# Fused attention, MLP and expert layer: when the experts' weight buffers are asked for again, and two scatters without a wait between them

## The chip, the cores and the metric

One core of one Trainium2 chip. The metric is the device time of one execution in microseconds (us), lower is better. Everything is float32 at the inputs and outputs.

## The reference, cut to what matters

Attention with a block mask over 4 x 8 x 576 x 64 gives 2304 rows of 512. A dense layer (512 to 2048 to 512, PReLU) follows, and then the part in which the change lies: eight experts (512 to 1024 to 512, ReLU), of which each row visits the one with the largest logit.

```python
def _moe2_ref(x, w_gate, w1, w2):
    N, D = x.shape
    E = w_gate.shape[1]
    logits = x @ w_gate
    expert_idx = np.argmax(logits, axis=1)
    probs = np.exp(logits - logits.max(-1, keepdims=True))
    probs /= probs.sum(-1, keepdims=True) + 1e-09
    gate_w = probs[np.arange(N), expert_idx]
    out = np.zeros((N, D), dtype=np.float32)
    for e in range(E):
        mask = expert_idx == e
        if not mask.any():
            continue
        h = np.maximum(x[mask] @ w1[e], 0.0)
        out[mask] = gate_w[mask, None] * (h @ w2[e])
    return out
```

## The kernel before, in words

Attention and the dense layer fill the first 651 us of the profile; a planner (class `Plan`) orders their instructions, and the change does not touch it. The dense layer's results go to a DRAM tensor `x2`, 256 rows at a time in nine groups. After each group `Route` finds every row's expert, its place in that expert's list and its gate value, and POOL scatters (row number, gate value) into the DRAM tensor `info` with two indirect DMAs of 128 places each (`Route.scatter`, L853). The last group's routing runs inside the first expert tile: its steps stand in a dictionary that `Route.steps` returns (L878), by the number of half-finished products after which they are called.

`Experts.run` (L1156) takes the experts in order of size, r = 0, 1, 2, ... Expert r's rows come in tiles: `big(r, j)` does 256 rows (`tile256`, L1037), `remainder(r)` the rest with 128 or 64 rows, and `only(r)` an expert of at most 128 rows (`tile128`, L1066, or `tile64`, L1104). How many rows an expert has is known on the chip alone, so `tc.If` branches choose, and all five engines take each branch. In the profiled run the expert of rank 0 took tiles j = 0 to 4 and a remainder of 128, rank 1 two tiles and a remainder of 64, rank 2 one tile and a remainder of 64, rank 3 one tile of 128, rank 4 one of 64, and the rest had no rows.

For a tile, `fetch(r, j)` (L990) has SP load 256 entries of `info` into a small tile `it` (for j > 0 also into `rem`), and POOL gather the rows of `x2` that `it` names into `xg`, 128 rows per indirect DMA. `xprep` (L999) turns them with four transposes on PE (`Tx`) and splits them into a high and a low part (ACT copies, DVE subtracts: `cxh`, `cxl`). Then PE multiplies in three passes (`pass3`): first layer into `l` (or `H`), ReLU into `hh` and `hl`, second layer into `Y`, ACT scales it into `yo`, and POOL scatters `yo` to the output rows.

An expert's weights are 16 blocks of 128 x 512 float32, 256 KB each. SP loads them into 16 buffers `raw0` to `raw15` (`wload`, L970, its DMA at L977), and `conv(r, i)` (L984) makes a high part of a block on ACT and a low part on DVE (`e`). Blocks of the next expert but one are loaded while those of the next are converted: `load_next(r)` (L1179) asks for all 16 of expert r + 2 and stands behind the whole tile in which expert r + 1's blocks are converted. Each load waits until DVE has converted the block that is in the buffer. The conversions are jobs: a tile's `step` calls (L1017) take one or more of them between pieces of the products, and with `more=1` also one entry of the list `ahead`, which `nexts` (L1172) makes: the gathers' `xprep` of the next tile, the `fetch` of the next expert's first tile, and its `xprep`. A 256-row tile with jobs has 16 steps: eight in the first layer, four in each half of the second. `tile128` and `tile64` have few steps with several jobs each.

Rank 1's blocks are asked for by an entry of `ahead` in the first tile (L1257), which stands ahead of the branch `few0` (L1266; 640 rows or fewer) and the branch `many0` (L1273; more). SP runs its instructions in the order in which they are written. It waits at each for what that one needs, and all its DMAs go out on the one queue q1. Where a branch is not taken, the block that takes its place waits for the DMAs of SP's eight lanes that are under way.

Of the kernel before, what the change touches and what calls it, by code (L numbers as in the profile page):

```python
# [778 lines left out]
class Route:  # L779
# [53 lines left out]
    def place(A, rk):  # L833
        nc, K, g, GE, oh, ex, sm, small = A.nc, A.K, A.g, GT * E, A.oh, A.ex, A.sm, A.small
        run = K.run[g % 2]
        for i in range(GT):
            nc.vector.tensor_add(run[:, i + 1], run[:, i], rk[:, E * i:E * i + E])
        nc.vector.tensor_copy(K.run[(g + 1) % 2][:, 0], run[:, GT])
        pos, sl, A.si = small("pos", [GT, E]), small("sl", [GT]), small("si", [GT], I32)
        nc.vector.tensor_add(pos, run[:, 0:GT], rk[:, GE:2 * GE].rearrange("p (i e) -> p i e", e=E))  # L840
        nc.vector.tensor_mul(pos, pos, oh)
        nc.vector.reduce_sum(sl, pos, axis=AX.X)
        nc.vector.tensor_copy(A.si, sl)

        A.ig, gx, ge = small("ig", [GT, 2], I32), small("gx", [GT, E]), small("ge", [GT])
        nc.gpsimd.tensor_scalar(A.ig[:, :, 0], K.pid, g * G, None, op0=ALU.add)
        nc.vector.tensor_scalar_add(sm, sm, 1e-9)
        nc.vector.tensor_mul(gx, ex, oh)
        nc.vector.reciprocal(sm, sm)
        nc.vector.reduce_sum(ge, gx, axis=AX.X)  # L850
        nc.vector.tensor_mul(A.ig[:, :, 1].bitcast(F32), ge, sm)

    def scatter(A, i):  # L853
        A.nc.gpsimd.indirect_dma_start(out=A.ml.info, out_offset=IOA(ap=A.si[:, i:i + 1], axis=0), in_=A.ig[:, i, :], in_offset=None)

    def steps(A, psp, xts):
# [20 lines left out]

        return {2: turns, 4: pick, 7: rank, 8: lambda: (A.scatter(0), A.scatter(1))}  # L878

# [50 lines left out]
class Experts:  # L930
# [59 lines left out]
    def fetch(A, r, j, base, rows=NT + 1):  # L990
        it = A.itile(r, j)
        src = A.info[ds(base + 2 * P * j, 2 * P), :].rearrange("(h p) c -> p h c", p=P)
        A.nc.sync.dma_start(it, src)
        if j:
            A.nc.sync.dma_start(A.rem, src)
        for h in range(2):
# [69 lines left out]
    def tile128(A, n, W, it, x, step):  # L1066
# [21 lines left out]

        step(5)
        l1(0, range(4))  # L1090
        step(3)
        l1(1, (0, 1))
        turn(0)
        step(2)
        l1(1, (2, 3))
        Y = A.psp.tile("H", f"Y{n}")
        l2((0, 1))
        turn(1)
        step(7, 2)
        l2(range(2, 8))  # L1100
# [55 lines left out]
    def run(A, base, last, order, order_all):  # L1156
# [21 lines left out]

        def load_next(r):  # L1179
            if r < E - 2:  # L1180
                A.load_raws(r + 2, reg(0, r + 2, E - 1))

        def big(r, j, b, jobs=(), nb=None):
            more = A.TOP[r] > 2 * P * (j + 1)
# [3 lines left out]
            if more:  # L1188
                A.fetch(r, j + 1, b)
            A.body(r, j, 2 * P, jobs, nexts(r, j + 1, b if more else None, nb))  # L1190
            if jobs:
                load_next(r)

# [20 lines left out]
        def remainder(r):  # L1214
# [8 lines left out]
            sized(P if A.TOP[r] > 2 * P + 64 else 64, lambda k: n > P - 1 + k, go)  # L1223

        def only(r, nb):

            jobs = [lambda: A.fetch(r + 1, 0, nb)] + [lambda i=i: A.conv(r + 1, i) for i in range(16)] if r < E - 1 else []
            if r < E - 2:
                jobs[-1] = lambda: (A.conv(r + 1, 15), load_next(r))

            def go(size):
                hint(f"more{r}", ns[r] > P)
                A.body(r, 0, size, jobs, xpreps(r + 1, 0) if jobs else (), cond=ns[r + 1] > 0 if jobs else None)
# [21 lines left out]
        for f in [lambda: A.fetch(0, 1, base), order_all, known] + [lambda i=i: late(i) for i in range(FIRST, 16)]:  # L1255
            at[max(at) + 1] = f
        ahead = [lambda: None] * 2 + [counts, lambda: A.load_raws(1, hold["e1"]), lambda: None] + xpreps(0, 1)  # L1257
        A.body(0, 0, 2 * P, [], ahead, at)
# [3 lines left out]

        def convs(r):
            return [lambda i=i: A.conv(r, i) for i in range(16)]

        with A.tc.If(n0 <= 5 * P, label="few0"):  # L1266
            with A.tc.If(n0 > 3 * P) as c:
                big(0, 1, base, convs(1), nb)
            with c.Else():
                for f in [lambda: A.fetch(1, 0, nb)] + convs(1) + xpreps(1, 0) + [lambda: load_next(0)]:  # L1270
                    f()
            hint("many0", n0 > 5 * P)
        with A.tc.If(n0 > 5 * P, label="many0"):  # L1273
            big(0, 1, base)
            big(0, 2, base, convs(1), nb)
            bigs(0, 3, base)
        remainder(0)
        with ExitStack() as st:  # L1278
            for r in range(1, E):
                base = nb  # L1280
                st.enter_context(A.tc.If(ns[r] > 0))
                nb = reg(2, r + 1, (E - 1) * NT) if r < E - 1 else None
                jobs = convs(r + 1) if r < E - 1 else []
                with A.tc.If(ns[r] <= P, label=f"less{r}"):  # L1284
                    only(r, nb)
                if r < E - 1:
                    st.enter_context(A.tc.If(ns[r] + P * ns[r + 1] > P))
                with A.tc.If(ns[r] > P, label=f"more{r}"):  # L1288
                    big(r, 0, base, jobs, nb)
                    bigs(r, 1, base)  # L1290
# [3 lines left out]
def moe_kernel(tc, qk, v, qke, ve, w_in, w_out, alpha, w_gate, w1, w2, out):  # L1294
    nc = tc.nc
    with ExitStack() as ctx:
# [135 lines left out]
        ex.s = od.pl.tile([P, 256], F32, name="s")  # L1432
        todo = Route(ml, NG - 1, lambda i: ex.yo[i], {}).steps(banks, [ex.xg[:, i] for i in range(GT)])
        ex.run(hold["base"], todo, od, lambda: od.all(K.run[(NG - 1) % 2][0:1, GT]))
# [52 lines left out]
```

## Time and profile before

| what | value |
|---|---|
| median of 3 runs | 951.15 us (950.98 to 956.93) |
| the profiled execution | 951.48 us; its span from first to last instruction 949.7 us |
| mean granted TensorE clock | 0.976 |
| busy: PE, DVE, ACT, POOL | 94%, 53%, 43%, 31% of the span |
| experts' part | from 651.6 us on; last product ends at 936.6 us, last scatter starts at 937.9 us |

How to read it: a row of a timeline has the start, the duration, the engine, the line, the operation, output<-inputs and, in brackets, how long the engine was idle before and what ended that. "SPq" is SP's instruction queue: its duration is the issuing of a DMA, not its transfer. Names stand without buffer numbers, so `xg` is either half of the gathered rows and `raw` any of the 16 buffers. The row of a window has the busy time of each engine in it, the granted TensorE clock (1.00 is 2.4 GHz, 0.50 is 1.2 GHz), the mean busy share of the 16 DMA engines and GB/s.

### The profile page before, as it was taken

How to read it: one execution, taken by the hardware profiler on the slowest of the kernel's cores; microseconds unless marked ns; L12 is line 12 of the kernel's file. 1: busy time of each engine (PE TensorE's matmuls, PEld its weight loads, DVE VectorE, ACT ScalarE, POOL GpSimd, SP SyncE). 2: the span in 40 equal slices, each digit the busy share in tenths (PEclk: the TensorE clock that was granted, in tenths of full speed). 3: DMA queues.
4: the chain of work that ended last, by engine and by line, in shares of the span. 5: the costliest groups of instructions: out<-in, count | busy, mean ns of one | idle time of the engine just before them, and what ended most of it. 6: DMA issues, size and time to landing. Idle time of an engine off the chain costs nothing. (4 is left out here: it accounts for less than half of the span.)

```text
span 949.7 us, 17897 instructions
## 1 busy us (share of the span) xinstructions
PE 892.8 (94%) x6329; PEld 763.4 (80%) x6329; DVE 499.5 (53%) x1215; ACT 409.7 (43%) x1037; POOL 294.1 (31%) x312
## 2 busy tenths in 40 slices
PE   7999989999999999999999999999889998998884
PEld 6656658888888888888999999979778987988763
DVE  4999896657546555656434353546215211613450
ACT  7777765454455446454312121223215222523451
POOL 1555673323343432443222223241212111111110
PEclk9999999999999999999999999999999998998997
DMA  8981002312302122001001010043526211622551
GB/s 340 362 317 56 23 20 74 75 48 71 75 28 76 48 59 94 28 27 36 31 2 45 1 45 2 23 123 101 170 88 222 68 47 56 198 62 80 169 163 62
DMA packets 46267, 85.80 MB, mean 90 GB/s; under 512 B 12191, under 2 KB 18991, under 8 KB 46128
## 3 DMA queue, kind: packets, MB, share of 16 engines
q1 hardware_dynamic: 35264, 64.20, 20.7%
q0 software_dynamic: 4240, 11.56, 3.8%
q10 hardware_dynamic: 6624, 8.39, 2.5%
q8 instruction: 63, 1.03, 0.5%
q14 instruction: 76, 0.62, 0.2%
HBM read 70.85 MB, written 13.67 MB: 89 GB/s over the span
## 5 line engine op out<-in xcount | busy, mean ns | idle before, releaser
L693 PE MATMUL l<-xh,wi 128*128 128x256 f32 x1024 | 206.0, 287 | 0.0
L693 PEld LDWEIGHTS l<-xh,wi 128*128 128x128 f32 x1024 | 167.0, 191 | 4.2 <-issue 0.5
L721 PE MATMUL acc<-wo,gh 128*128 128x512 f32 x512 | 167.3, 408 | 0.0
L693 PE MATMUL l<-xl,wi 128*128 128x256 f32 x512 | 145.0, 283 | 0.1
L699 POOL TENSOR_TENSOR gl<-t,gh 128x256 fp32r<-128x256 f32 x103 | 78.5, 764 | 193.3 <-ACT gh L696 158.4
L671 DVE TENSOR_SCALAR t<-l,al 128x256 f32<-128x256 f32 x128 | 61.9, 484 | 141.6 <-PE l L693 136.1
L696 ACT CAST gh<-t 128x256 fp32r<-128x256 f32 x124 | 50.4, 406 | 186.1 <-DVE t L672 105.3
L529 POOL TENSOR_SCALAR P<-P,sm 128x256 f32<-128x256 f32 (+4 forms) x66 | 78.4, 1195 | 107.7 <-ACT gh L696 39.8
L721 PE MATMUL acc<-wo,gl 128*128 128x512 f32 x256 | 101.0, 394 | 2.8 <-POOL gl L699 2.8
L693 PEld LDWEIGHTS l<-xl,wi 128*128 128x128 f32 x512 | 97.8, 191 | 4.0 <-issue 0.5
L721 PEld LDWEIGHTS acc<-wo,gh 128*128 128x128 f32 x512 | 87.0, 191 | 11.3 <-issue 0.5
L478 DVE TENSOR_REDUCE nb<-S 128x1 f32<-128x256 f32 (+4 forms) x160 | 70.1, 477 | 40.2 <-PE S L455 25.9
L523 ACT COPY F<-PT 128x384 f32<-128x384 f32 (+2 forms) x124 | 57.6, 479 | 52.8 <-PE PT L518 51.5
L495 ACT ACTIVATE P<-S,nb 128x128 f32<-128x128 f32 (+3 forms) x128 | 67.0, 531 | 14.3 <-DVE nb L478 12.9
L518 PE MATMUL PT<-ident,P 128*128 128x128 f32 (+1 forms) x400 | 64.7, 281 | 6.4 <-DVE xo L572 3.9
L518 PEld LDWEIGHTS PT<-ident,P 128*128 128x128 f32 (+1 forms) x400 | 45.9, 141 | 20.0 <-issue 3.5
L721 PEld LDWEIGHTS acc<-wo,gl 128*128 128x128 f32 x256 | 48.2, 188 | 14.7 <-POOL gl L699 3.7
L1031 PE MATMUL l<-cxh,e 128*128 128x256 f32 x320 | 58.3, 282 | 1.0 <-ACTq L1266 1.0
L1031 PE MATMUL Y<-e,hh 128*128 128x512 f32 x176 | 57.2, 406 | 0.0
L672 DVE SCALAR_TENSOR_TENSOR t<-l,t 128x256 f32<-128x256 f32 x128 | 54.3, 425 | 4.4
L988 DVE TENSOR_TENSOR e<-raw,e 128x512 fp32r<-128x512 f32 x68 | 43.9, 686 | 21.4 <-ACT e L987 17.8
L562 PE MATMUL o<-F,v 128*64 128x128 f32 (+2 forms) x832 | 53.4, 264 | 0.0
(373 smaller groups left out, 1677.8 us busy)
## 6 DMA issues: line engine op xcount, KB each, us to landing
raw<-in_moe_w_dram SPq DMA_DIRECT2D x96, 256.0 KB
qk<-in_qk_dram SPq DMA_DIRECT2D x16, 608.0 KB
rawi<-in_moe_w_in_dram SPq DMA_DIRECT2D x16, 512.0 KB
rawo<-in_moe_w_out_dram SPq DMA_DIRECT2D x16, 512.0 KB
v<-in_v_dram SPq DMA_DIRECT2D x16, 320.0 KB
x<-y ACTq DMA_DIRECT2D x16, 256.0 KB
xr<-xT SPq DMA_DIRECT2D x7, 512.0 KB
qe<-in_qke_dram SPq DMA_DIRECT2D x8, 256.0 KB
```

The lines of the kernel that those rows point to most:

```text
L478: nc.vector.tensor_reduce(pl["nb", p, c][:, 2 * k + j:2 * k + j + 1], pl[Ss[j]][:, a:b], axis=AX.X, op=ALU.max, negate=True)
L495: nc.scalar.activation(pl[x][:, a:b], pl[Ss[j]][:, a:b], AF.Exp, bias=nb, scale=1.0, accum_out=pl["sm", p, c][:, 2 * k + j:2 * k + j + 1])
L518: nc.tensor.transpose(pl[t][0:w, k], pl[x][:, P * k:P * k + w], A.K.ident)
L523: f(pl[F][:, 0:n], pl[t][:, 0:n])
L529: (nc.gpsimd if on == "POOL" else nc.vector).tensor_scalar(y, y, pl["sm", p, c][:, k:k + 1], None, op0=ALU.mult)
L562: nc.tensor.matmul(y, lhsT=v[0:w, 2 * kc + h], rhs=f, start=kc == 0, stop=kc == c, skip_group_check=True)
L671: nc.vector.tensor_scalar(pl[out], x, 0.0, A.K.al[:, f:f + 1], op0=ALU.min, op1=ALU.mult)
L672: nc.vector.scalar_tensor_tensor(pl[out], x, 0.0, pl[out], op0=ALU.max, op1=ALU.add)
L693: nc.tensor.matmul(pl[l][:, 0:G], lhsT=a[:, c], rhs=b, start=k == 0 and j == 0, stop=k == 3 and j == 2)
L699: (nc.gpsimd if on == "POOL" else nc.vector).tensor_sub(pl[gl], pl[t], pl[gh].bitcast(F32))
L721: nc.tensor.matmul(pl[acc], lhsT=x[:, c], rhs=w, start=f == 0 and j == 0, stop=f == 15 and j == 2)
L1031: A.nc.tensor.matmul(ps, lhsT=x[a], rhs=w[b], start=first and q == 0, stop=last and q == 2)
```

## The change

Three edits, and one of numbers.

1. The last group's scatters. The row numbers of its second half are written between the two scatters (`token(1)`), the dependence of the second scatter on the first is taken away (both write `info`, at other places), and the loads of `info` for tile (0, 1) get a dependence on both scatters.
2. Rank 1's blocks (`load_raws(1, ...)`) are no longer asked for in the first tile but in `big(0, 1)` behind the branch, after that tile's `fetch`.
3. `load_next` is gone. Each job converts a block and asks at once for the block of the next expert but one in the same buffer (`convs`, `one`).
4. `tile128` takes its jobs in portions of 4, 1, 3 and 9 in place of 5, 3, 2 and 7, and two branch hints are set in other places; the branch behind `only` gets a label (`on`) and a hint.

```diff
--- before.py
+++ after.py
@@ -843,15 +843,21 @@
         nc.vector.tensor_copy(A.si, sl)
 
         A.ig, gx, ge = small("ig", [GT, 2], I32), small("gx", [GT, E]), small("ge", [GT])
-        nc.gpsimd.tensor_scalar(A.ig[:, :, 0], K.pid, g * G, None, op0=ALU.add)
+        if g < NG - 1:
+            nc.gpsimd.tensor_scalar(A.ig[:, :, 0], K.pid, g * G, None, op0=ALU.add)
+        else:
+            A.token(0)
         nc.vector.tensor_scalar_add(sm, sm, 1e-9)
         nc.vector.tensor_mul(gx, ex, oh)
         nc.vector.reciprocal(sm, sm)
         nc.vector.reduce_sum(ge, gx, axis=AX.X)
         nc.vector.tensor_mul(A.ig[:, :, 1].bitcast(F32), ge, sm)
 
+    def token(A, i):
+        A.nc.gpsimd.tensor_scalar(A.ig[:, i, 0:1], A.K.pid[:, i:i + 1], A.g * G, None, op0=ALU.add)
+
     def scatter(A, i):
-        A.nc.gpsimd.indirect_dma_start(out=A.ml.info, out_offset=IOA(ap=A.si[:, i:i + 1], axis=0), in_=A.ig[:, i, :], in_offset=None)
+        return A.nc.gpsimd.indirect_dma_start(out=A.ml.info, out_offset=IOA(ap=A.si[:, i:i + 1], axis=0), in_=A.ig[:, i, :], in_offset=None)
 
     def steps(A, psp, xts):
 
@@ -875,7 +881,14 @@
             A.rank(rk)
             A.place(rk)
 
-        return {2: turns, 4: pick, 7: rank, 8: lambda: (A.scatter(0), A.scatter(1))}
+        def scatters():
+
+            tc, A.sent = A.ml.tc, [A.scatter(0)]
+            A.token(1)
+            A.sent.append(A.scatter(1))
+            tc.declare_no_dep(A.sent[1].ins, A.sent[0].ins, reason="other places")
+
+        return {2: turns, 4: pick, 7: rank, 8: scatters}
 
 
 class Order:
@@ -990,9 +1003,12 @@
     def fetch(A, r, j, base, rows=NT + 1):
         it = A.itile(r, j)
         src = A.info[ds(base + 2 * P * j, 2 * P), :].rearrange("(h p) c -> p h c", p=P)
-        A.nc.sync.dma_start(it, src)
+        got = [A.nc.sync.dma_start(it, src)]
         if j:
-            A.nc.sync.dma_start(A.rem, src)
+            got.append(A.nc.sync.dma_start(A.rem, src))
+        for x in got if (r, j) == (0, 1) else ():
+            for y in A.last.sent:
+                A.tc.add_manual_dep(x.ins, y.ins.name, mybir.DependencyInfo(mybir.DependencyClass.Sync, mybir.DependencyReason.DATA), reason="places")
         for h in range(2):
             A.nc.gpsimd.indirect_dma_start(out=A.xg[:, h], out_offset=None, in_=A.x2[0:rows, :], in_offset=IOA(ap=it[:, h, 0:1], axis=0))
 
@@ -1086,17 +1102,17 @@
             for f in fs:
                 A.pass3(Y, [t[:, f % 4 // 2, P * (f % 2):P * (f % 2) + P] for t in A.hs[f // 4]], W[8 + f], f == 0, f == 7)
 
-        step(5)
+        step(4)
         l1(0, range(4))
-        step(3)
+        step(1)
         l1(1, (0, 1))
         turn(0)
-        step(2)
+        step(3)
         l1(1, (2, 3))
         Y = A.psp.tile("H", f"Y{n}")
         l2((0, 1))
         turn(1)
-        step(7, 2)
+        step(9, 2)
         l2(range(2, 8))
         nc.scalar.activation(A.yo[0], Y, AF.Copy, scale=it[:, 0, 1:2].bitcast(F32))
         A.scatter(A.yo[0], it)
@@ -1176,20 +1192,16 @@
                 fs += [lambda: None] * (6 - len(fs)) + xpreps(r + 1, 0)
             return fs
 
-        def load_next(r):
-            if r < E - 2:
-                A.load_raws(r + 2, reg(0, r + 2, E - 1))
-
-        def big(r, j, b, jobs=(), nb=None):
+        def big(r, j, b, jobs=(), nb=None, raws=None):
             more = A.TOP[r] > 2 * P * (j + 1)
 
             if A.TOP[r] > 2 * P * (j + 1) + P and (r, j) != (0, 1):
                 hint(f"rest{r}_{j + 1}", ns[r] > 2 * P * (j + 1) + P)
             if more:
                 A.fetch(r, j + 1, b)
+            if raws is not None:
+                A.load_raws(1, raws)
             A.body(r, j, 2 * P, jobs, nexts(r, j + 1, b if more else None, nb))
-            if jobs:
-                load_next(r)
 
         def bigs(r, j, b):
             if A.TOP[r] > 2 * P * j + P:
@@ -1222,14 +1234,25 @@
 
             sized(P if A.TOP[r] > 2 * P + 64 else 64, lambda k: n > P - 1 + k, go)
 
+        def convs(r):
+
+            e = reg(0, r + 1, E - 1) if r < E - 1 else None
+
+            def one(i):
+                A.conv(r, i)
+                if e is not None:
+                    A.wload(r + 1, e, i, A.raws[i])
+
+            return [lambda i=i: one(i) for i in range(16)]
+
         def only(r, nb):
 
-            jobs = [lambda: A.fetch(r + 1, 0, nb)] + [lambda i=i: A.conv(r + 1, i) for i in range(16)] if r < E - 1 else []
-            if r < E - 2:
-                jobs[-1] = lambda: (A.conv(r + 1, 15), load_next(r))
+            jobs = [lambda: A.fetch(r + 1, 0, nb)] + convs(r + 1) if r < E - 1 else []
+            if jobs:
+                jobs[-1] = lambda f=jobs[-1]: (f(), hint(f"more{r}", ns[r] > P))
 
             def go(size):
-                hint(f"more{r}", ns[r] > P)
+                hint(f"on{r}" if jobs else f"more{r}", ns[r + 1] > 0 if jobs else ns[r] > P)
                 A.body(r, 0, size, jobs, xpreps(r + 1, 0) if jobs else (), cond=ns[r + 1] > 0 if jobs else None)
 
             with A.tc.If(ns[r] <= 64) as c:
@@ -1254,24 +1277,21 @@
 
         for f in [lambda: A.fetch(0, 1, base), order_all, known] + [lambda i=i: late(i) for i in range(FIRST, 16)]:
             at[max(at) + 1] = f
-        ahead = [lambda: None] * 2 + [counts, lambda: A.load_raws(1, hold["e1"]), lambda: None] + xpreps(0, 1)
+        ahead = [lambda: None] * 2 + [counts] + [lambda: None] * 2 + xpreps(0, 1)
         A.body(0, 0, 2 * P, [], ahead, at)
         nb = hold["nb"]
         ns = hold["n"]
         n0 = ns[0]
 
-        def convs(r):
-            return [lambda i=i: A.conv(r, i) for i in range(16)]
-
         with A.tc.If(n0 <= 5 * P, label="few0"):
             with A.tc.If(n0 > 3 * P) as c:
-                big(0, 1, base, convs(1), nb)
+                big(0, 1, base, convs(1), nb, hold["e1"])
             with c.Else():
-                for f in [lambda: A.fetch(1, 0, nb)] + convs(1) + xpreps(1, 0) + [lambda: load_next(0)]:
+                for f in [lambda: A.fetch(1, 0, nb), lambda: A.load_raws(1, hold["e1"])] + convs(1) + xpreps(1, 0):
                     f()
             hint("many0", n0 > 5 * P)
         with A.tc.If(n0 > 5 * P, label="many0"):
-            big(0, 1, base)
+            big(0, 1, base, raws=hold["e1"])
             big(0, 2, base, convs(1), nb)
             bigs(0, 3, base)
         remainder(0)
@@ -1280,13 +1300,12 @@
                 base = nb
                 st.enter_context(A.tc.If(ns[r] > 0))
                 nb = reg(2, r + 1, (E - 1) * NT) if r < E - 1 else None
-                jobs = convs(r + 1) if r < E - 1 else []
                 with A.tc.If(ns[r] <= P, label=f"less{r}"):
                     only(r, nb)
                 if r < E - 1:
-                    st.enter_context(A.tc.If(ns[r] + P * ns[r + 1] > P))
+                    st.enter_context(A.tc.If(ns[r] + P * ns[r + 1] > P, label=f"on{r}"))
                 with A.tc.If(ns[r] > P, label=f"more{r}"):
-                    big(r, 0, base, jobs, nb)
+                    big(r, 0, base, convs(r + 1) if r < E - 1 else [], nb)
                     bigs(r, 1, base)
                     remainder(r)
 
@@ -1430,7 +1449,8 @@
         od.pl = ctx.enter_context(tc.tile_pool(name="raw", bufs=1))
         ex.rawtiles(od.pl, 16 - NR)
         ex.s = od.pl.tile([P, 256], F32, name="s")
-        todo = Route(ml, NG - 1, lambda i: ex.yo[i], {}).steps(banks, [ex.xg[:, i] for i in range(GT)])
+        ex.last = Route(ml, NG - 1, lambda i: ex.yo[i], {})
+        todo = ex.last.steps(banks, [ex.xg[:, i] for i in range(GT)])
         ex.run(hold["base"], todo, od, lambda: od.all(K.run[(NG - 1) % 2][0:1, GT]))
```

The order in which instructions stand on an engine, before and with the change, at three places. On POOL, in the first expert tile, the two scatters of the last group (`ig` holds row number and gate value, `si` the places); before:

```order
L846 TENSOR_SCALAR ig8_8078<-pid_90 128x2
L854 DMA info_60<-ig8_8078,si8_8073 18432x2 x2
L997 DMA xg_6016<-x2_58,it11_6014 128x512 x2
L1247 TENSOR_LOAD odri_8127
L1170 REGISTER_ALU
```

and with the change:

```order
L857 TENSOR_SCALAR ig8_8078<-pid_90 128x1
L860 DMA info_60<-ig8_8078,si8_8073 18432x2
L857 TENSOR_SCALAR ig8_8078<-pid_90 128x1
L860 DMA info_60<-ig8_8078,si8_8073 18432x2
L1013 DMA xg_6016<-x2_58,it11_6014 128x512 x2
```

One instruction of POOL came between the scatters; the gathers of tile (0, 1) follow as before.

On SP, in the branch `many0`, from tile (0, 2)'s fetch to the conversions in that tile; `it10`, `it11` and `it01` are the lists of tiles (0, 2), (0, 3) and (1, 0). Before (the 16 loads of rank 1's blocks stand ahead of the branch, and are not in this piece):

```order
L1273 COMPARE_AND_BRANCH
L993 DMA it10_6013<-info_60 128x2x2
L995 DMA rem_6015<-info_60 128x2x2
L993 DMA it11_6014<-info_60 128x2x2
L995 DMA rem_6015<-info_60 128x2x2
L993 DMA it01_6012<-info_60 128x2x2
L977 DMA raw0_6031<-in_moe2_w1_dram 128x512
L977 DMA raw1_6032<-in_moe2_w1_dram 128x512
```

With the change, first the end of the 16 loads, which now stand between the lists of (0, 2) and (0, 3), and then the place of `it01`:

```order
L990 DMA raw15_7979<-in_moe2_w2_dram 128x512
L1006 DMA it11_6014<-info_60 128x2x2
L1008 DMA rem_6015<-info_60 128x2x2
L990 DMA raw0_6031<-in_moe2_w1_dram 128x512
...
L990 DMA raw9_7973<-in_moe2_w2_dram 128x512
L990 DMA raw10_7974<-in_moe2_w2_dram 128x512
L1006 DMA it01_6012<-info_60 128x2x2
L990 DMA raw11_7975<-in_moe2_w2_dram 128x512
```

The list of the next expert's first tile stood ahead of all 16 loads, and now stands behind eleven of them (`raw0` to `raw10`). In tiles (1, 0) and (2, 0) the order is the same: before, `it` of the next expert and then `raw0`; now `raw10`, `it`, `raw11`.

On DVE, in `tile128` of rank 3 (`e0` is a converted block, `hl0` the low part of the first half of the hidden values); before:

```order
L988 TENSOR_TENSOR e0_3_7785<-raw3_6034,e0_3_7785 128x512
L1020 UNCONDITIONAL_BRANCH x2
L1020 COMPARE_AND_BRANCH
L988 TENSOR_TENSOR e0_4_7811<-raw4_7968,e0_4_7811 128x512
L988 TENSOR_TENSOR e0_5_7832<-raw5_7969,e0_5_7832 128x512
L988 TENSOR_TENSOR e0_6_7851<-raw6_7970,e0_6_7851 128x512
L1020 UNCONDITIONAL_BRANCH x2
L1083 TENSOR_TENSOR hl0_6024<-Th3_0_128+_0_14668,hh0_6023 128x512
```

and with the change:

```order
L1001 TENSOR_TENSOR e0_3_7785<-raw3_6034,e0_3_7785 128x512
L1036 UNCONDITIONAL_BRANCH x2
L1099 TENSOR_TENSOR hl0_6024<-Th3_0_128+_0_14756,hh0_6023 128x512
L1036 COMPARE_AND_BRANCH
L1001 TENSOR_TENSOR e0_4_7811<-raw4_7968,e0_4_7811 128x512
```

Ahead of `hl0` stood seven conversions, and now four.

## Rows read from the trace of the kernel before

**Rows 1.** The page: span, and part 1, busy time of each engine.

```profile
span 949.7 us, 17897 instructions
...
PE 892.8 (94%) x6329; PEld 763.4 (80%) x6329; DVE 499.5 (53%) x1215; ACT 409.7 (43%) x1037; POOL 294.1 (31%) x312
```

**Rows 2.** Waits of PE, 651 to 950 us: total, times, longest.

```profile
PE Tx L1004 <- DMA xg<-x,it: 6.8, 4, 4.1
...
PE Y_128+_14687 L1031 <- DVE hl L1083: 2.4, 1, 2.4
```

**Rows 3.** Timeline of PE: transposes of gathered rows, each expert tile's next.

```profile
676.75 0.63 PE L1004 MATMUL Tx<-ident,xg 128*128 128x128 f32 x4 [2.15 <-DMA xg<-x,it]
...
700.06 1.09 PE L1004 MATMUL Tx<-ident,xg 128*128 128x128 f32 x4 [4.10 <-DMA xg<-x,it]
...
727.68 0.30 PE L1004 MATMUL Tx<-ident,xg 128*128 128x128 f32 x1 [0.37 <-DMA xg<-x,it]
...
733.74 0.27 PE L1004 MATMUL Tx<-ident,xg 128*128 128x128 f32 x1
...
824.67 0.27 PE L1004 MATMUL Tx<-ident,xg 128*128 128x128 f32 x1
...
889.33 0.27 PE L1004 MATMUL Tx<-ident,xg 128*128 128x128 f32 x1
```

**Rows 4.** Timeline of POOL: the last scatters of places, gathers of rows.

```profile
662.42 1.06 POOL L854 DMA_INDIRECT info<-ig,si  x1 [11.81 <-DVE odnf L893]
666.30 1.26 POOL L854 DMA_INDIRECT info<-ig,si  x1 [2.82 <-DMA info<-ig,si]
673.37 0.98 POOL L997 DMA_INDIRECT xg<-x,it  x1 [5.81 <-DMA it<-info]
...
696.54 0.99 POOL L997 DMA_INDIRECT xg<-x,it  x1 [13.07 <-DMA it<-info]
...
720.67 0.97 POOL L997 DMA_INDIRECT xg<-x,it  x1 [0.30 <-issue]
...
817.68 0.95 POOL L997 DMA_INDIRECT xg<-x,it  x1 [14.11 <-PE Tx L1004]
...
833.63 0.99 POOL L997 DMA_INDIRECT xg<-x,it  x1 [3.50 <-SPq L1196]
```

**Rows 5.** Timeline of SP's queue: lists of places, and loads of weight blocks.

```profile
676.04 11.93 SPq L977 DMA_DIRECT2D raw<-in_moe_w_dram  x16
693.94 0.39 SPq L993 DMA_DIRECT2D it<-info  x1
...
718.10 0.37 SPq L993 DMA_DIRECT2D it<-info  x1
...
730.88 0.33 SPq L977 DMA_DIRECT2D raw<-in_moe_w_dram  x1
...
821.82 0.55 SPq L977 DMA_DIRECT2D raw<-in_moe_w_dram  x1
...
830.37 0.03 SPq L993 DMA_DIRECT2D it<-info  x1
...
886.47 0.33 SPq L977 DMA_DIRECT2D raw<-in_moe_w_dram  x1
```

**Rows 6.** Windows, tiles (0, 1) and (0, 3), two stretches after waits: engines' busy time, clock, DMA.

```profile
681.64:710.90 29.26, 25.16 (x152) 22.28 (x153) 4.48 (x7) 4.26 (x7) 3.99 (x4) 0.94 0.44 149
...
735.93:759.49 23.56, 23.56 (x156) 21.28 (x155) 6.46 (x11) 5.95 (x10) 3.99 (x4) 1.00 0.23 69
...
700.06:703.50 3.44, 3.44 (x11) 2.79 (x12) 1.02 (x2) 0.59 (x1) 0.00 (x0) 0.51 0.12 49
...
915.40:918.50 3.10, 3.07 (x10) 2.58 (x11) 1.17 (x2) 0.11 (x1) 0.00 (x0) 0.51 0.98 303
```

**Rows 7.** Timeline of DVE, the tile of 128 rows of rank 3.

```profile
910.46 4.31 DVE L988 TENSOR_TENSOR e<-raw,e 128x512 fp32r<-128x512 f32 x7 [3.36 <-ACT yo L1075]
914.69 0.69 DVE L1083 TENSOR_TENSOR hl<-Th_128+_0_14668,hh 128x512 fp32r<-128x512 f32 x1
```

## The prediction

> **What bounds the kernel now.** I read the page first. PE is busy for 94% of the span [rows 1], so the change can win only where PE stops, and loses wherever it makes PE stop. The waits of PE come next. In the experts' part one wait is larger than any other: transposes that wait for gathered rows, 6.8 us in four waits, the longest 4.1 [rows 2]. The only stop by conversions is one of 2.4 us at the low part of rank 3's hidden values [rows 2]; no stop is put down to a weight block that has not landed. The reader is to see in this that loading weights earlier is worth nothing by itself: the loads keep up with the conversions already, and no product waits for one.
>
> Then PE's timeline at those transposes [rows 3], and behind each of them POOL's gather [rows 4] and SP's list [rows 5], because the chain is list, gather, transpose. Tile (0, 1): 2.15 us of idle PE before the transpose at 676.75. Tile (0, 2): 4.10 us before 700.06. The windows give what the second stop cost in all: tile (0, 1), in which PE prepares (0, 2), took 29.26 us, where tile (0, 3), with the same products and no stop, took 23.56 [rows 6]. The difference, 5.70, is 4.10 of idle time and 1.6 of slow clock: right behind the stop the granted clock is 0.51, near the level of 1.2 GHz, for 3.44 us [rows 6], which loses 3.44 x 0.49 = 1.7.
>
> **The change part by part.** The scatters. The second starts at 666.30 after 2.82 us of waiting for the first one's landing [rows 4]. Without that wait and with one small instruction of POOL between, it starts about 0.5 us after the first ends at 663.48, near 664.0, so 2.3 us earlier. The list, the gather at 673.37 and the landing before 676.75 follow it one by one, so all move by 2.3. PE came to this transpose 2.15 us before the rows. The stop goes: -2.15 us (between -1.5, should the token's instruction take longer than I put, and -2.15). What is late next is PE itself.
>
> Rank 1's loads behind the branch. Before, SP issues 16 loads from 676.04 to 687.97, then stands at the branch not taken, and issues tile (0, 2)'s list at 693.94, six us later [rows 5]; the gather follows at 696.54 and the transpose waits until 700.06. With the change SP has nothing under way at the branch but two short lists, and asks for (0, 2)'s rows ahead of the loads. It can do that near 678 to 680; even at 684 the rows would land before PE comes to the transpose at 696. The stop and its slow clock go: -5.7 us (-4.1 to -5.8). The 16 loads now begin some 4 us later than 676.04. They took 18 us to the end of the wait at 693.94, so they would be complete near 698, and the first conversion of rank 1 comes in tile (0, 2), behind 710.90 less the 8 us gained, 703. This cover is 5 us; if it were gone, conversions and not PE would be late, and they have 25 us of that tile to catch up.
>
> Portions of `tile128`. Rank 3's tile had seven conversions ahead of `hl`, 4.31 us for seven [rows 7], 0.62 each. With four, `hl` comes 1.85 us earlier and most of the 2.4 us stop goes. The slow stretch behind it, 3.10 us at 0.51 [rows 6], is worth another 1.5. Two more conversions, 1.2 us, stand behind the second turn instead, on the engines for which the last tile of 64 rows waits. So 1.85 + 1.5 - 1.2 = 2.1 us gained (0.6 to 3.3). The hints and the label I put at nothing: the branches whose stops the waits show at ranks 1 and 2 are not those that get a hint.
>
> Refilling at once. Here the price lies. Before, SP had issued the next expert's list long before its rows were wanted: at 718.10 [rows 5], for a transpose at 733.74 [rows 3]. The gather then waited only for its buffer: POOL's at 817.68, for the transpose at 824.67, had been held by the previous transpose and not by a list [rows 3, 4]. With the change this list stands behind the load of block 10, which waits for conversion 10. In the trace of before the load of block 11 is what SP issued next behind that conversion, at 730.88, 821.82 and 886.47 [rows 5] in the three tiles with 16 steps, and the list takes its place. From a list's issue to its gather 2.6 us pass with nothing in front (693.94 to 696.54), and 3.3 with a block load just issued in front (830.37 to 833.63) [rows 4, 5]. From the gather's start to the transpose that it holds up 3.4 to 3.5 us pass (673.37 to 676.75; 696.54 to 700.06), and 7.0 where a burst of block loads runs beside it (720.67 to 727.68) [rows 3, 4]. There is a load in front, so I take 3.3; the loads behind it come one by one as conversions end and not in a burst, so I take 3.5. Rows are there 6.8 us after the list: at 737.7, 828.6 and 893.3. PE wants them at 733.74, 824.67 and 889.33 [rows 3]. It stands still for 3.9 us at each of the three. By the low ends (2.6 + 3.4) it would be 3.1, by the high ends (3.3 + 7.0) 7.4. Behind stops of 4.1 and 2.4 us the clock fell [rows 2, 6], so I add 1.7 at each; the bounds are nothing, as after the stop of 2.15, and 1.7. That is 3 x (3.9 + 1.7) = +16.8 us, from 9.3 to 27.3. Nothing covers it: the transposes stand in PE's own order, and the next products cannot pass them. The block loads themselves start at about the times they did, since conversions set these.
>
> A rule speaks against this edit too. The trace shows a list that came 0.7 us later with one load in front [rows 4, 5]. The Trainium skill, "DMA: Bandwidth & Descriptors", section "Queues, rings and completion order", says that each DMA engine takes the descriptors of one ring in ring order, so that a list would wait for every block asked for ahead of it on SP's queue. By that rule tile (0, 2), where eleven blocks would be asked for between 718 and 731, could have one more of them before the list, some 0.8 us by a rough estimate, and the sum would be 0.8 us higher. I keep the row's 0.7.
>
> The sum: -2.15 - 5.7 - 2.1 = -9.95 gained, +16.8 lost, so +6.85 on the profiled execution's 951.48 us (the span of 949.7 and 1.8 around it): 958.3. The median of the three runs is 951.15, 0.3 below it; I forecast 958.0 us, 0.7% above the median. A measurement of this kernel can tell about 1% from no change.
>
> **The rivals.** First, that the late list costs nothing: the rows land within the time that PE still has, and only the gains stay. That gives 951.5 - 9.95 = 941.5, and 941.2 against the median, 1.0% faster. For it speaks that the gathers held by their buffer, as at 817.68, were ready without a stop 7 us later. Against it: from conversion 10's load PE has only 2.9 us to the transpose (821.82 to 824.67), and no list with its gather took less than 6.0.
>
> Second, and on the other side: the list and its gather run at the speed of the loaded queue. In all three tiles five more block loads are released within 10 us of the list, and the one gather of before that ran beside a burst took 7.0 us [rows 3, 4]. At 7.4 us for each stop and 1.7 for the clock the loss is 27.3 and the time 968.5 against the median. It decides the sign of what can be measured from where a stop with its slow clock costs 6.5 us in place of 5.6: then the loss is 19.5 and the time 960.7, 1% over. Against it: outside the burst in tile (0, 2) the loads come one or two at a time.
>
> Between these, the gains could be smaller than I put, by 3 us if the last part's reordering is worth the low end and the token takes longer; that shifts the time within the forecast's own range.
>
> **How the numbers follow.** My forecast, stops of 3 to 4.5 us with or without all of the slow clock, has 0.58; it spans 950 to 960. The first rival has 0.09, the second 0.33. Faster by over 1% (below 941.6) is nearly the first rival alone: 0.08, since at its full price it only just passes that line. Slower by over 1% is the second: 0.34. Same is the rest, 0.58. The range of 947 to 967 leaves out the first rival and the far end of the second, not quite 2 in 10.
>
> **What would show it.** Right: PE's waits of transposes for `xg` no longer at tiles (0, 1) and (0, 2), but three new ones of 3 to 5 us in tiles (0, 2), (1, 0) and (2, 0), just ahead of the transposes of ranks 1, 2 and 3, with a granted clock near 0.5 behind them; on SP's timeline the list right behind the load of block 10, and POOL's gathers of these rows released by the list and not by a transpose. Tile (0, 1) at 23.6 us. `hl` of rank 3 within 1 us of PE. Wrong: if those three gathers still start when the previous transpose frees the buffer, or if PE's stops stay under 2 us, my main term is gone; if tile (0, 1) stays near 29 us, the branch was not what held SP's list.

## The result, and the profile after

The changed kernel takes 958.34 us (median, 954.30 to 963.82), the kernel before 951.63 us in the same comparison. The ratio is 1.0078, interval [1.0058, 1.0098]. The forecast of 958.0 us stands, and so does the forecast that the change stays within 1%: the interval puts the loss at 0.6% to 1.0%. The profiled execution took 956.94 us, and its span is 955.1, 5.4 more than before.

The page of the changed kernel, span and part 1 [rows 1]:

```profile
span 955.1 us, 17920 instructions
...
PE 894.6 (94%) x6329; PEld 764.7 (80%) x6329; DVE 499.9 (52%) x1215; ACT 409.8 (43%) x1037; POOL 295.2 (31%) x313
```

Waits of PE from 640 to 956 us (total, times, longest) [rows 2]:

```profile
PE Tx L1020 <- DMA xg<-x,it: 12.1, 4, 3.5
PE H_64+_0_15831 L1130 <- DVEq L1307: 3.3, 1, 3.3
...
PE l L1047 <- PEq L1286: 1.9, 1, 1.9
...
PE Y_128+_14780 L1047 <- DVE hl L1099: 0.9, 1, 0.9
```

There are four waits of transposes as before, but they are others. PE's timeline, the first product behind the branch `few0` (680.06) and the transposes that waited [rows 3]:

```profile
680.06 0.36 PE L1047 MATMUL l<-cxh,e 128*128 128x256 f32 x1 [1.91 <-PEq L1286]
...
721.20 0.63 PE L1020 MATMUL Tx<-ident,xg 128*128 128x128 f32 x4 [1.87 <-DMA xg<-x,it]
...
734.12 0.63 PE L1020 MATMUL Tx<-ident,xg 128*128 128x128 f32 x4 [3.21 <-DMA xg<-x,it]
...
827.78 0.73 PE L1020 MATMUL Tx<-ident,xg 128*128 128x128 f32 x4 [3.54 <-DMA xg<-x,it]
...
896.42 1.09 PE L1020 MATMUL Tx<-ident,xg 128*128 128x128 f32 x4 [3.43 <-DMA xg<-x,it]
```

The stops before tiles (0, 1) and (0, 2) are gone. The last three rows are the transposes of ranks 1, 2 and 3, which had no wait in [rows 3]; the row at 721.20 belongs to tile (0, 3). SP's queue shows the lists: first (0, 2)'s, then those of the three ranks, each right behind the load of block 10, the eleventh of its tile (shown for rank 1) [rows 5]:

```profile
680.09 0.39 SPq L1006 DMA_DIRECT2D it<-info  x1
...
712.78 14.36 SPq L990 DMA_DIRECT2D raw<-in_moe_w_dram  x11
727.39 0.38 SPq L1006 DMA_DIRECT2D it<-info  x1
...
821.25 0.38 SPq L1006 DMA_DIRECT2D it<-info  x1
...
890.04 0.38 SPq L1006 DMA_DIRECT2D it<-info  x1
```

And POOL's timeline has the second scatter of places, then the gathers that answer those three lists [rows 4]:

```profile
663.78 1.05 POOL L860 DMA_INDIRECT info<-ig,si  x1 [0.28 <-POOL ig L857]
...
730.42 0.96 POOL L1013 DMA_INDIRECT xg<-x,it  x1 [13.29 <-DMA it<-info]
...
824.20 0.95 POOL L1013 DMA_INDIRECT xg<-x,it  x1 [20.17 <-DMA it<-info]
...
892.93 0.95 POOL L1013 DMA_INDIRECT xg<-x,it  x1 [19.36 <-DMA it<-info]
```

In [rows 4] the gather at 817.68 was released by the previous transpose; here all three are released by the list. Windows by tile give what that cost: first four of the kernel before, tiles (0, 2), (1, 0), (2, 0) and rank 3's (columns as in [rows 6]: length, busy time of PE, PEld, DVE, ACT and POOL, granted clock, DMA share, GB/s):

```profile
710.90:735.93 25.03, 24.50 (x161) 21.61 (x160) 14.00 (x23) 13.16 (x24) 5.89 (x6) 1.00 0.64 210
...
799.89:826.86 26.97, 26.97 (x160) 24.61 (x161) 14.07 (x23) 12.58 (x23) 4.93 (x5) 0.89 0.59 188
864.54:895.17 30.63, 27.22 (x160) 24.64 (x161) 15.98 (x26) 14.27 (x26) 5.95 (x6) 0.89 0.56 175
905.92:925.65 19.73, 15.25 (x67) 11.45 (x65) 13.01 (x22) 12.74 (x24) 3.92 (x4) 0.91 0.63 191
```

and of the changed kernel, tiles (0, 1), (0, 2), (1, 0), (2, 0) and rank 3's:

```profile
680.06:705.11 25.05, 25.05 (x152) 22.79 (x153) 4.48 (x7) 4.26 (x7) 3.09 (x4) 0.93 0.64 211
705.11:736.34 31.23, 26.14 (x162) 22.65 (x160) 14.01 (x23) 13.25 (x24) 6.31 (x6) 0.95 0.54 169
...
800.40:831.58 31.18, 27.64 (x161) 24.63 (x161) 14.71 (x24) 12.57 (x23) 4.89 (x5) 0.89 0.52 163
869.18:903.32 34.14, 27.85 (x161) 24.65 (x161) 15.97 (x26) 14.27 (x26) 5.76 (x6) 0.90 0.51 155
914.30:931.99 17.69, 13.46 (x67) 10.47 (x65) 13.01 (x22) 12.70 (x24) 4.23 (x4) 1.00 0.64 199
```

The tiles that carry refills became 6.20, 4.21 and 3.51 us longer; tile (0, 1) became 4.21 shorter (29.26 in [rows 6]), and rank 3's 2.04 shorter.

### The profile page after: what moved, and what is told of

Read it like the earlier page. It is cut to its first block, busy times and chain, and to the rows that moved or that the text cites. A ratio compares the mean times of both kernels' runs of the same rounds, so it can differ in the third digit from the quotient of the medians.

```text
span 955.1 us, 17920 instructions
## 1 busy us (share of the span) xinstructions
PE 894.6 (94%) x6329; PEld 764.7 (80%) x6329; DVE 499.9 (52%) x1215; ACT 409.8 (43%) x1037; POOL 295.2 (31%) x313
```

## The experiments

All compute the full result. Ratios are to the kernel before, whose medians in these comparisons are 950.6 to 950.8 us. My theory: the loss is the place of the next expert's list on SP's queue, and the refilling itself neither wins nor loses. The rivals: contention of gathers with block loads, and a cost of the refilling itself.

**The list first.** The changed kernel, with that list ahead of the tile's conversions and loads; the gather stays where it was.

```diff
+            if nb is not None:
+                A.places(r + 1, nb)
             A.body(r, j, 2 * P, jobs, nexts(r, j + 1, b if more else None, nb))
...
-                fs += [lambda: A.fetch(r + 1, 0, nb)]
+                fs += [lambda: A.gather(r + 1, 0)]
```

> The changed kernel, with one thing moved: the list of the next expert's first tile is asked for ahead of that tile's block loads again, the gather stays where it was. My theory (the list stands behind the load of block 10, which waits for a conversion): PE's stops of 3.2, 3.5 and 3.4 us before the transposes of ranks 1, 2 and 3 fall below 0.5 us each, POOL's gathers start when the previous transpose frees the buffer, and 11 to 14 us go, so 944 to 948 us, ratio to the kernel before 0.992 to 0.996. Rival (the block loads beside the gather make it slow, wherever the list stands): stops of 2 us or more stay, ratio 1.004 or more.

Measured: 941.74 us, ratio 0.9892 [0.9847, 0.9937]. Its one wait of a transpose, and its windows of tiles (0, 2), (1, 0) and (2, 0):

```profile
PE Tx L1028 <- DMA xg<-x,it: 1.1, 1, 1.1
```

```profile
703.94:729.68 25.74, 24.50 (x162) 21.60 (x160) 14.01 (x24) 13.16 (x24) 6.38 (x6) 1.00 0.63 205
793.48:817.73 24.25, 24.25 (x161) 21.87 (x161) 14.01 (x23) 12.57 (x23) 5.44 (x5) 1.00 0.67 203
855.34:883.58 28.24, 24.49 (x160) 21.90 (x161) 15.97 (x26) 14.27 (x26) 5.95 (x6) 1.00 0.66 194
```

The three stops are gone, though block loads run beside these gathers too; but the gathers have 7 us here until PE wants their rows (808.54 to 815.54 in tile (1, 0)), so this run alone does not tell how slow loads can make a gather. What is left, 1.1 us, is tile (0, 3)'s. Moving one list takes 958.34 - 941.74 = 16.6 us away, more than the 11 to 14 that I had put: besides the stops the slow clock goes, as all three windows are at 1.00. This version beats both kernels.

**Loads back.** The changed kernel without edit 3: all 16 loads stand behind the tile again.

```diff
+            if jobs:
+                load_next(r)
...
-            def one(i):
-                A.conv(r, i)
-                if e is not None:
-                    A.wload(r + 1, e, i, A.raws[i])
-
-            return [lambda i=i: one(i) for i in range(16)]
+            return [lambda i=i: A.conv(r, i) for i in range(16)]
```

> The changed kernel with the refilling undone: all 16 loads are written behind the tile in which the blocks are converted, as before; the scatters, the loads of rank 1 behind the branch and the portions of the 128-row tile are kept. My theory (refilling at once gains nothing by itself, as conversions set when a buffer is free): within 1.5 us of the kernel with the list in front, ratio to the kernel before 0.991 to 0.996. Rival (earlier loads are worth something, and the stops hid it): 3 us or more slower than that kernel.

Measured: 943.32 us, 0.9910 [0.9874, 0.9946], with no wait of a transpose over 0.3 us. It is 1.6 us above the list first, where I had put at most 1.5, and the two intervals overlap: with the list in a good place, refilling at once is worth nothing that these runs can tell.

**Refilling alone.** The kernel before with edit 3 alone (its lines of the diff: `convs`, `one`, no `load_next`).

> The kernel before with the refilling alone: each job converts a block and asks for the next one in its buffer. My theory: three stops of PE of 3 to 4.5 us before the transposes of ranks 1, 2 and 3, and 10 to 15 us lost, ratio 1.010 to 1.016; tile (0, 1) stays at 29 us with its stop of 4.1. Rival (the stops come from the other edits, which start the loads of tile (0, 2) earlier): stops under 1.5 us, ratio 0.998 to 1.004.

Measured: 971.14 us, 1.0186 [1.0138, 1.0235]. The direction is as expected, the loss larger, and tile (0, 1) did not keep its stop of 4.1 us. The stops before ranks 1, 2 and 3 are 3.75, 3.53 and 3.40 us, like those of the changed kernel, but two waits look strange:

```profile
PE Tx L1004 <- DMA xg<-x,it: 16.1, 6, 3.8
PE l L1031 <- PEq L1266: 4.7, 1, 4.7
```

The stop at the branch `few0` was 0.99 us before. So either refilling costs something at the branch, or that stop belongs to something else; later runs tell.

**Behind the branch alone.** The kernel before with edit 2 alone (`load_raws(1, raws)` in `big` behind `fetch`).

> The kernel before with rank 1's loads behind the branch alone. My theory (SP stood at the branch not taken until the loads had landed): the stop of 4.1 us in tile (0, 1) goes, SP issues the list of (0, 2) before 684 us, tile (0, 1) takes 23.5 to 25.5 us, ratio 0.994 to 0.997. Rival (the list of (0, 2) is held by the branch itself or by the buffer): a stop of 3 us or more stays, ratio 0.999 to 1.001.

Measured: 945.64 us, 0.9945 [0.9915, 0.9975]. Tile (0, 1) takes 23.53 us at full clock, and (0, 2)'s transposes have no stop; the branch costs 1.63. The window of tile (0, 1), and (0, 2)'s list on SP's queue, 0.3 us after the tile's first product (put before 684):

```profile
684.63:708.16 23.53, 23.53 (x152) 21.28 (x153) 4.48 (x7) 4.26 (x7) 3.36 (x4) 1.00 0.68 224
```

```profile
684.96 0.38 SPq L993 DMA_DIRECT2D it<-info  x1
```

**The list behind block 8, and behind block 12.** The changed kernel; first the list alone moves up, then the list and its gather move down.

```diff
-            fs = [lambda: None] + xpreps(r, j) if b is not None else []
+            fs = [lambda: None] + xpreps(r, j) if b is not None else [lambda: None] * 3
             if nb is not None:
-                fs += [lambda: A.fetch(r + 1, 0, nb)]
+                fs[1] = lambda f=fs[1]: (A.places(r + 1, nb), f())
+                fs += [lambda: A.gather(r + 1, 0)]
```

```diff
-                fs += [lambda: A.fetch(r + 1, 0, nb)]
-                fs += [lambda: None] * (6 - len(fs)) + xpreps(r + 1, 0)
+                fs += [lambda: None] * (5 - len(fs)) + [lambda: A.fetch(r + 1, 0, nb)] + xpreps(r + 1, 0)
```

> The changed kernel, but the list of the next expert's first tile stands behind the load of block 8 in place of block 10; POOL's gather stays where it is. If the list's own lateness sets the stops (my theory: stop = list's issue + 6.4 us or so, less the time at which PE wants the rows), each of the three stops before the transposes of ranks 1, 2 and 3 becomes about 2 us shorter, since in the trace of before the load of block 9 was issued some 2.1 us ahead of that of block 11 in tile (1, 0): stops of 1 to 1.5 us, some 6 to 8 us off the changed kernel with part of the slow clock, near 951 us, ratio to the kernel before 0.997 to 1.003. If the loads that run beside the gather set the stops (rival: contention), the gather stands where it stood and seven loads follow in place of five: stops stay at 3.2 to 3.5 us and the ratio near 1.008.

> The changed kernel, but the list of the next expert's first tile and its gather stand behind the load of block 12 in place of block 10. If the list's own lateness sets the stops, each grows by the time between the loads of blocks 11 and 13, about 1.5 us in tile (1, 0) before: stops of 4.5 to 5.5 us, some 5 to 7 us above the changed kernel, near 964 us, ratio to the kernel before 1.012 to 1.017. If contention with the loads behind the list sets them (rival), there are three of these in place of five: stops no longer than 3.5 us and the ratio at or under 1.008.

Measured: 951.54 us, 1.0012 [0.9987, 1.0037], and 968.56 us, 1.0179 [1.0121, 1.0237]. The list and gather of rank 2 on SP's and POOL's timelines, and PE's at its transposes, first with the list behind block 8, then behind 12:

```profile
814.52 0.38 SPq L1004 DMA_DIRECT2D it<-info  x1
...
818.13 1.06 POOL L1009 DMA_INDIRECT xg<-x,it  x1 [14.64 <-PE Y_256+_0_11242 L1055]
819.50 1.24 POOL L1009 DMA_INDIRECT xg<-x,it  x1 [0.30 <-DMA raw<-in_moe_w_dram]
...
821.88 0.63 PE L1028 MATMUL Tx<-ident,xg 128*128 128x128 f32 x4
825.18 0.63 PE L1028 MATMUL Tx<-ident,xg 128*128 128x128 f32 x4 [1.27 <-DMA xg<-x,it]
```

```profile
829.15 0.38 SPq L1006 DMA_DIRECT2D it<-info  x1
...
833.44 0.97 POOL L1013 DMA_INDIRECT xg<-x,it  x1 [4.88 <-DMA it<-info]
...
837.07 1.09 PE L1020 MATMUL Tx<-ident,xg 128*128 128x128 f32 x4 [6.45 <-DMA xg<-x,it]
```

| list stands | stops of ranks 1, 2, 3 (both halves) | median |
|---|---|---|
| ahead of all | none | 941.74 |
| behind block 8 | 1.06, 1.27, 1.56 | 951.54 |
| behind block 10 | 3.21, 3.54, 3.43 | 958.34 |
| behind block 12 | 6.29, 6.45, 6.10 | 968.56 |

The later the list, the longer each stop, and the fewer loads follow it. Contention as the setter of the changed kernel's three stops falls: with seven loads behind the list they are short, and with three long. Behind block 12 they grew more than I had put, 2.9 us and not 1.5, since these lists also took 3.9 to 4.4 us to their gathers (829.15 to 833.44), where the changed kernel's took 2.9 to 3.0.

What is left behind block 8 is not the list's, though its size is the 1 to 1.5 us that I had put. The list moved further than I put: it went out 14.7 us into tile (1, 0), where behind block 10 it was 20.9, so 6 us earlier and not 2 (2.8 in tile (2, 0)), and for ranks 2 and 3 the first half's rows were there in time. The profile has all three gathers released by a product of PE and not by the list, and the stops of ranks 2 and 3 stand before the second half, whose gather took 5.7 us (6.1 for rank 3) to its transposes with block loads beside it. The gathers for tile (0, 1) show the same: with rank 1's loads behind the branch alone, and so no block loads beside it, the second half was there within 4.1, and where the 16 loads ran beside it PE had to wait for it in four kernels, 4.6 to 5.5 us from its start. So the agreement of this number is luck, and loads beside a gather do cost something; they did not set the stops of 3.2 to 3.5.

**Refilling alone, list first.** The kernel before with edit 3 and the list ahead, as in the first experiment.

> The kernel before with edit 3 alone, but with the list of the next expert's first tile ahead of the tile's conversions and loads. Edit 3 alone lost more (1.0186) than the stops of its three transposes are worth; its trace also had a stop of 4.7 us at the first branch. If the list's place is all that costs (my theory), nothing is left of the loss: ratio 0.995 to 1.004, no stop before the transposes of ranks 1 to 3, and the branch's stop at 1 to 2 us. If refilling at once costs by itself, at the branch or by its burst of loads in tile (0, 2) (rival), the branch keeps 4 us or more, tile (0, 3) begins with a stop over 1 us, and the ratio is 1.005 to 1.010.

Measured: 954.18 us, 1.0029 [1.0004, 1.0055]. No stop before ranks 1 to 3, nor before (0, 3); but the branch keeps its 4.70 us, which the rival foresaw; the rest of the rival, a stop in tile (0, 3) and a ratio over 1.005, did not come. In its trace the experts' part is no longer than before (284.25 us from PE's first product to its last, 285.03 before), so where its 0.3% goes stays open. By this pair, with and without the list first, the list's place costs 971.14 - 954.18 = 17.0 us.

**Portions alone.** The kernel before with the four numbers of edit 4's `step` calls.

```diff
-        step(5)
+        step(4)
...
-        step(3)
+        step(1)
...
-        step(2)
+        step(3)
...
-        step(7, 2)
+        step(9, 2)
```

> The kernel before with the portions of the tile of 128 rows alone (4, 1, 3, 9 in place of 5, 3, 2, 7). Theory: the stop of 2.4 us at the low part of rank 3's hidden values falls to 1 us or less, and what is won there is partly given back at the tile of 64 rows behind it: 1 to 3 us, ratio 0.997 to 0.999, from the start of rank 3's tile to the last product 27.7 to 30 us where before took 30.7. Rival: what is won at the first turn is lost at the second or in the tile of 64 rows: the same 30.7 us, with a stop of 3 us or more at the hidden values of the last tile.

Measured: 951.00 us, 0.9997 [0.9970, 1.0024]. The stop at `hl` falls from 2.4 to 1.0, the one ahead of the last tile's first product grows from 2.1 to 3.4, and rank 3's tile to the last product takes 29.38 us where before took 30.71. A gain of 1.3 us in one trace is not to be seen in the times.

**Scatters alone.** The kernel before with edit 1.

> The kernel before with edit 1 alone: the second half's row numbers written between the two scatters of places, the second scatter free of the first, the lists of tile (0, 1) behind both. Theory: the list of tile (0, 1) and its gather come 2 us or more earlier, the stop of 2.15 us before that tile's first transpose goes, and nothing else changes: 949 us, ratio 0.996 to 0.999, with the stop of 4 us before the transposes of tile (0, 2) still there. Rival: what is won there is lost at the branch right behind it, where SP and the other engines stand until the loads under way have landed: the stop at the branch grows from 1 us to 3, and the ratio is 0.999 to 1.002.

Measured: 948.79 us, 0.9976 [0.9946, 1.0006]. Here is the answer to the strange branch. PE's waits:

```profile
PE l L1047 <- PEq L1282: 5.0, 1, 5.0
PE Tx L1020 <- DMA xg<-x,it: 1.1, 2, 0.8
```

The stop at the branch is 5 us without any refilling, and the transposes of (0, 2) no longer stop, against my theory; the rival had the branch's stop grow, to 3 us. Over all kernels:

| kernel | stop at `few0` | before (0, 2) |
|---|---|---|
| before | 0.99 | 4.10 |
| portions alone | 1.09 | 2.99 |
| refilling alone | 4.67 | none |
| refilling alone, list first | 4.70 | none |
| scatters alone | 5.05 | none |
| loads behind the branch (all six) | 1.63 to 2.11 | none |

In the first five kernels rank 1's loads stand ahead of the branch, and PE stands 4.1 to 5.1 us in all, nearly all of it at the branch or most of it one tile later; with the loads behind it is 1.6 to 2.1. So it is the loads ahead of the branch that cost this, not the refilling. Why PE's branch is quick in two of the five kernels stays open.

## Why the prediction was right

**Scatters, -2.15.** Right in place and size. The second scatter started at 663.78 (put at 664.0), and the stop of 2.15 us before tile (0, 1) is gone. From the experts' start to the branch the gain is 1.22, since the branch behind it took 0.9 more, which I had put nowhere. Alone the edit's gain is not shown: its interval includes 1.

**Loads behind the branch, -5.7.** Right in mechanism, too large in size. The list of (0, 2) went out at 680.09 (put near 678 to 680), and its stop is gone. But tile (0, 1) takes 25.05 us and not 23.6: the new stop of 1.91 at the branch is followed by a stretch at 1.2 GHz, here in a window of the changed kernel:

```profile
681.39:684.80 3.41, 3.41 (x18) 3.41 (x18) 0.00 (x0) 0.27 (x1) 0.61 (x1) 0.50 0.49 121
```

It loses 3.41 x 0.5 = 1.7. So the tile gained 4.21. In the run of this edit alone the same tile came to 23.53, and its ratio of 0.9945 is a gain of about 5.2 us, near the 5.7. With the scatters the two terms measure -5.4 where I summed -7.85; the missed part is the branch, whose stop I took as given, and the slow clock behind it. The 16 loads began at 682.41, 6.4 us later than before and not 4, and no product waited for them.

**Portions, -2.1.** The two windows at the end (rank 3's tile, and the last tile up to the last product) give -2.04 and -0.97, 3.0 in all; the second I had not put. PE waits 0.9 us for `hl`, with four conversions ahead of it as put:

```profile
918.71 2.50 DVE L1001 TENSOR_TENSOR e<-raw,e 128x512 fp32r<-128x512 f32 x4 [3.23 <-issue]
921.13 0.68 DVE L1099 TENSOR_TENSOR hl<-Th_128+_0_14756,hh 128x512 fp32r<-128x512 f32 x1
```

The stop ahead of the last tile grew from 2.10 to 3.33, which is the 1.2 I had put for two conversions more. Part of the gain is the clock, 1.00 in rank 3's window where it was 0.91. Alone the edit is worth nothing measurable, so I would not claim the term.

**Refilling at once, +16.8.** Right in mechanism, in place and nearly in size. The list went from SP to the gather in 3.03, 2.95 and 2.89 us (I took 3.3, from a gather whose row in [rows 4] has it released by SP and not by its list), and from the gather to the transposes 3.70, 3.58 and 3.49 passed (I took 3.5), hardly more than the 3.4 to 3.5 of [rows 3, 4]; so loads beside these gathers cost 0.3 us at most. The stops were 3.2 to 3.5 and not 3.9, and the tiles grew by 6.20 + 4.21 + 3.51 = 13.9. Two sizes were off, in opposite directions. The slow clock, put at 1.7 for each stop, was less against the kernel before: for the same products PE was busy 24.50 + 26.97 + 27.22 = 78.7 us in the three windows before and 26.14 + 27.64 + 27.85 = 81.6 after, 2.9 more and not 5.1, because two of these tiles had lost clock already. And tile (0, 3)'s transposes stopped for 1.87 us (0.37 in [rows 3]), which I had not foreseen. Their gather started 9.3 us into tile (0, 2), at 714.45, and took 6.75 us to the transposes, where before it started 8.5 us in and took 5.9; the refills go out from 712.78 on, 7.7 us into the tile, where before the 16 loads began 8.5 us in. That the refills cause it is likely and not shown: the two kernels without refilling and with the loads behind the branch have no such stop, but refilling alone with the list first has none either, and the portions alone have stops of 0.45 and 0.81 us there without refilling.

Undoing only the list's place gives the term without that mix: 16.6 us by one pair of medians, 17.0 by the other; the ratios give 17.7 and 14.9, and their intervals leave some 5 us either way. That this meets the 16.8 so closely is luck, since the forecast put too much into the stops, and the changed kernel pays more in slow clock against the list first (full clock in all three tiles, PE busy 73.2 us) than against before.

**The sum.** By windows: -1.22 - 4.21 + 13.92 - 2.04 - 0.97 is +5.5; the rest of the experts' part adds 0.3 and its earlier start takes 0.4, which gives the 5.4 by which the last product is later. I had +6.85: the gains were put 1.5 us too large and the loss 2.9. These errors cancel in part, so that the median lies within 0.4 us of the forecast is luck too. The Trainium skill's rule that I weighed, that a DMA engine takes the descriptors of a ring in ring order ("DMA: Bandwidth & Descriptors", section "Queues, rings and completion order"), would by my rough estimate have added 0.8 us at tile (0, 2). That list took 3.03 us to its gather, 0.1 more than the others, so nothing of it shows there. The 3.9 to 4.4 us behind block 12 do point its way, as three loads went out there in the 2.2 us ahead of the lists of ranks 1 and 2, and one or two in the changed kernel; how much of it is the queue they do not tell.

**The rivals.** That the list costs nothing is refuted by the three stops; its price, 941.2, is what the kernel with the list first takes (941.74). The loaded queue, with stops of 7.4 us, did not come about behind block 10; the kernel with the list behind block 12 came to 968.56, by a later list.

## What to carry to other kernels

When a queue's instructions are each released by another engine's work, look at what small transfer stands behind them: a list of 2 KB that a gather and then the busiest engine wait for belongs ahead of the bulk, even if nothing else changes. Loads that already keep up won nothing that could be measured by being asked for earlier, so the price of such an edit is all in what it pushes back. And when a stop goes, look for it at the next join: what the loads ahead of the branch cost appeared at the branch in some kernels (4.7 to 5.1 us) and a tile later in others (3.0 to 4.1).

## What had not been expected

The stop of PE at the untaken block of `few0` varied from 0.99 to 5.05 us among kernels whose loads of rank 1 stand ahead of it, and stayed at 1.63 to 2.11 in those where nothing but short lists was under way. The Trainium skill, "Runtime: NRT & Kernel Launch", section "Instruction fetch mechanics", says that a taken branch whose target is not at hand forces a fetch by DMA; a fetch behind 16 block loads would fit the long stops, but not the short ones of before and of the portions alone, and no run here separates the fetch.

The clock did not follow the stops one to one. In the changed kernel, windows right behind the stop of 1.87 us in tile (0, 2) and behind those of ranks 1, 2 and 3:

```profile
721.20:724.80 3.60, 3.60 (x15) 2.79 (x16) 1.62 (x3) 1.10 (x2) 0.00 (x0) 0.66 0.67 260
734.12:737.60 3.48, 3.48 (x24) 3.16 (x25) 1.98 (x4) 2.09 (x4) 0.00 (x0) 1.00 0.31 120
...
827.78:831.58 3.80, 3.80 (x15) 3.11 (x15) 1.62 (x3) 1.10 (x2) 0.00 (x0) 0.55 0.33 126
896.42:899.90 3.48, 3.48 (x11) 2.81 (x12) 1.62 (x3) 1.10 (x2) 0.04 (x1) 0.51 0.36 127
```

Behind rank 1's stop of 3.21 us the clock stayed at 1.00, against the sign that I had named, and behind the shorter stop of 1.87 it fell. Tile (1, 0) ran at a mean of 0.89 in the kernel before and at 1.00 with the list first, behind a stop of 2.9 us at the branch ahead of it in both. Tile (0, 1) took 25.05 us behind a stop of 1.91 in the changed kernel and 23.53 behind one of 1.94 with the list first. A fixed price in slow clock for each stop, as I put it, is therefore an average at best.
